# Taking the last key tile of one attention pair head by head, in a stage where TensorE hands over to a dense product

## The chip, the cores and the metric

The kernel runs on one core of one Trainium2 chip. The metric is the device time of one execution in microseconds. The kernel counts as faster or slower only beyond 2%.

## The reference

Attention with a relative-position bias, then a mixer with a low-rank token mixing and a two-layer channel product (8 batches, 8 heads, 576 tokens, 64 per head; channel width 512, hidden 2048):

```python
scores = scale * q @ k.T + bias[bucket(|i - j|)]
attn   = softmax(scores)
x      = attn @ v                      # heads side by side: 576 x 512 per batch
u      = x + (x.T @ U @ V).T
out    = u + relu(u @ w_ch1) @ w_ch2
```

## The kernel before

Two heads make a pair; g counts pairs over all batches, so g = 0 to 3 is batch 0. For each pair the scores lie in PSUM with keys on partitions, ScalarE exponentiates them into `p_sb`, VectorE multiplies the band near the diagonal by the exponentiated bias (`band`), TensorE multiplies with v (`pv`, a column of ones giving the row sums), VectorE divides (`normalise`), and TensorE mixes (`mix_t`, then `mix_ut`, which also transposes). From the fifth pair on, matmuls of the dense product (`work.run`) fill TensorE. The end of batch 0 is written out by hand, each engine taking its instructions in this order:

```python
    kts(3, 3)                        # scores and exponential of key tile 3, both heads
    to_copy = fourth_transposes()
    bands(3, 4, 0, 1)
    normalise(2)
    to_copy[0]()
    for kt in (4, 0, 1):
        pv(3, kt, (0,))
    mix_t(2, nc.scalar.copy)
    bands(3, 2)
    for kt in (4, 0, 1):
        pv(3, kt, (1,))
    bands(3, 3)
    pvs(3, 2, 3)                     # tile 2 head 0, tile 2 head 1, tile 3 head 0, tile 3 head 1
    mix_ut(2, nc.scalar.copy)
    normalise(3)
    ready[0] = True
    work.run(0.64)                   # three matmuls of the dense product
    to_copy[1]()
    mix_t(3, nc.scalar.copy)
    mix_ut(3, nc.vector.tensor_copy)
    # ... then the loop over g = 4 to 31; in it, at g = 7, segment 0:
            work.even(...)                   # dense matmuls
            # ...
            pair_transposes(g + 1, 0)        # needs the q of batch 2, all four token tiles
```

The softmax here doesn't subtract the row's maximum and nothing guards it: scores larger than these inputs give would overflow.

## Time and profile before

| | before |
|---|---|
| time, first three runs | 409.9 us median (409.36 to 410.46) |
| profiled span | 408.0 us |
| TensorE / VectorE / ScalarE / GpSimd busy | 95% / 60% / 51% / 31% |
| stage: start of pair 2's mixing product to start of pair 3's | 34.51 to 37.34, 2.83 us |
| TensorE back in the dense product | 39.53 us |
| TensorE's wait for the q load of batch 2 | 1.30 us, ending at 70.68 us |

TensorE is the busy engine, but a share doesn't say which stretch sets the end. The chain of waits does: the prediction shows that up to 70.68 us it runs through transfers and GpSimd, and through TensorE only afterwards. Below, "the mark" is the start of pair 2's mixing product, just ahead of the edit, and "the stage" runs from the mark to the start of pair 3's mixing product. TensorE's timeline has both ends of the stage, and just ahead of the second end a dense matmul (the third of `work.run(0.64)`) that waits for ScalarE's copy of pair 2's `uT`:

```profile
34.51 0.44 PE L647 MATMUL acc<-xp,upad 128*128 128x128 bf16 x5
...
37.12 0.38 PE L372 MATMUL acc<-uT,w1b 128*128 128x512 bf16 x1 [0.24 <-ACT uT L704]
37.34 0.44 PE L647 MATMUL acc<-xp,upad 128*128 128x128 bf16 x5
```

### The profile page before, as it was taken

Reading aid. Unit: us, or ns where it says so; the run is one execution under the profiler, and the core shown is the slowest. Engines: PE = TensorE matmul, PEld = TensorE weight load, DVE = VectorE, ACT = ScalarE, POOL = GpSimd, SP = SyncE. Lnnn points to the kernel's source line nnn. Section 1 sums busy time; section 2 is a strip of 40 time slices with the busy share of each in tenths; the row PEclk is TensorE's granted clock in tenths of the full one; section 3 lists DMA queues with packets and bytes.
Section 4 is the critical chain, followed back from the end, with each engine's and each line's share of the span. In section 5 each row is a group of like instructions: output and inputs, shape, how many; then the busy total and the mean of one; then the engine's idle time right before and its main releaser. Section 6 shows DMA issues by size and latency. Waiting matters only on the chain.

```text
span 408.0 us, 9061 instructions
## 1 busy us (share of the span) xinstructions
PE 386.7 (95%) x3636; PEld 214.8 (53%) x3700; DVE 243.2 (60%) x554; ACT 207.0 (51%) x289; POOL 124.7 (31%) x179
## 2 busy tenths in 40 slices
PE   3888998999999999999999999999999999999995
PEld 1456555555555555555555555555555554444443
DVE  6867887757664675566755776568655832422321
ACT  5886644565654566557655665455555640220310
POOL 4948924454454045404540454040000000000000
PEclk9789999999999999999999999999999999999999
DMA  7999999999999599949995999499022003001012
GB/s 130 181 159 157 112 187 128 119 104 155 151 78 117 123 117 94 129 104 135 108 100 130 127 88 91 110 135 105 14 66 66 14 14 95 35 4 75 26 27 77
DMA packets 162754, 40.68 MB, mean 100 GB/s; under 512 B 151792, under 2 KB 157176, under 8 KB 162712
## 3 DMA queue, kind: packets, MB, share of 16 engines
q0 software_dynamic: 108416, 17.97, 62.2%
q1 hardware_dynamic: 53080, 21.22, 25.6%
q10 hardware_dynamic: 1216, 0.92, 0.7%
q8 instruction: 29, 0.48, 0.5%
q14 instruction: 13, 0.11, 0.1%
HBM read 37.84 MB, written 9.45 MB: 116 GB/s over the span
## 4 chain that ended last, share of the span: by engine, by line
PE 81%; DMA 10%; POOL 5%; issue 2%; DVE 1%; ACT 0%; ACTq 0%; POOLq 0%
PE acc L392 30%; PE acc L372 27%; PE o L611 10%; PE sc L524 7%; DMA w1b<-in_moe_w_ch_dram 5%; DMA w2b<-in_moe_w_ch_dram 4%; PE acc L647 2%; POOL v_bf L255 2%; POOL qb L265 1%; PE acc L663 1%; DMA qb<-in_q_dram 1%; PE sc L537 1%; PE sc L558 1%; POOL qb L255 1%; DMA gp_dram<-gp 1%
## 5 line engine op out<-in xcount | busy, mean ns | idle before, releaser
L533 ACT ACTIVATE p_sb<-sc 128x1024 bf16<-128x1024 f32 x128 | 124.6, 1021 | 101.3 <-PE sc L524 101.1
L392 PE MATMUL acc<-w2b,g 128*128 128x512 bf16 (+1 forms) x560 | 128.7, 373 | 2.3 <-DVE ob L401 0.5
L372 PE MATMUL acc<-uT,w1b 128*128 128x512 bf16 x484 | 116.3, 380 | 2.5 <-issue 0.6
L392 PEld LDWEIGHTS <-g 128*128 128x128 bf16 x592 | 55.2, 98 | 70.2 <-issue 11.7
L372 PEld LDWEIGHTS <-w1b 128*128 128x128 bf16 x576 | 53.3, 98 | 71.5 <-issue 13.1
L383 DVE TENSOR_SCALAR g<-acc 128x512 bf16<-128x512 f32 x94 | 64.7, 690 | 34.7 <-PE acc L372 31.7
L587 DVE TENSOR_TENSOR p_sb<-p_sb,eb 128x768 bf16<-128x768 bf16 (+3 forms) x160 | 69.8, 465 | 12.1 <-ACT p_sb L533 9.5
L381 ACT ACTIVATE g<-acc 128x512 bf16<-128x512 f32 x50 | 29.9, 598 | 59.8 <-PE acc L372 59.6
L611 PEld LDWEIGHTS <-p_sb 128*128 128x128 bf16 x1600 | 56.3, 98 | 6.9 <-issue 1.3
L611 PE MATMUL o<-v_bf,p_sb 128*128 128x65 bf16 x1500 | 58.3, 194 | 0.2 <-DVE p_sb L587 0.2
L401 DVE TENSOR_TENSOR ob<-acc,u_tok 128x512 f32<-128x512 f32 x32 | 22.1, 691 | 44.3 <-PE acc L392 39.4
L524 PE MATMUL sc<-qkT 64*128 64x512 bf16 x256 | 41.7, 395 | 1.3 <-ACT qkT L469 0.7
L914 POOL COPY gate<-xp 1x2 bf16<-1x2 bf16 x18 | 3.1, 175 | 121.7 <-DVE xp L636 121.7
L671 DVE TENSOR_TENSOR u_tok<-acc,xp 128x512 bf16<-128x512 f32 x32 | 22.1, 691 | 24.8 <-PE acc L663 24.7
L636 DVE TENSOR_TENSOR xp<-o,rcp 128x320 bf16<-128x320 f32 x60 | 29.5, 491 | 3.2
L255 POOL DMA_DIRECT2D v_bf<-in_v_dram x32 | 28.5, 915 | 2.0 <-DMA w1b<-in_moe_w_ch_dram 1.7
L255 POOL DMA_DIRECT2D qb<-in_q_dram x24 | 22.1, 921 | 5.0 <-DVE p_sb L587 5.0
L255 POOL DMA_DIRECT2D qb<-in_k_dram x24 | 21.9, 910 | 5.5 <-DMA w2b<-in_moe_w_ch_dram 3.5
L567 ACT ACTIVATE p_sb<-sc 128x640 bf16<-128x640 f32 x32 | 22.4, 698 | 0.4 <-PE sc L561 0.3
L550 ACT ACTIVATE p_sb<-sc 128x512 bf16<-128x512 f32 x32 | 19.1, 598 | 3.5 <-PE sc L537 1.2
L634 DVE RECIPROCAL rcp<-o 128x5 f32<-128x5 f32 x60 | 11.5, 191 | 14.0 <-PE o L611 13.3
L647 PEld LDWEIGHTS <-upad 128*128 128x128 bf16 x160 | 11.4, 98 | 7.8 <-DVE xp L636 0.7
(90 smaller groups left out, 257.5 us busy)
## 6 DMA issues: line engine op xcount, KB each, us to landing
out_dram<-ob SPq DMA_DIRECT2D x32, 256.0 KB, 2.3
v_bf<-in_v_dram POOLq DMA_DIRECT2D x32, 128.0 KB, 5.7
qb<-in_q_dram POOLq DMA_DIRECT2D x27, 128.0 KB, 4.4
qb<-in_k_dram POOLq DMA_DIRECT2D x27, 128.0 KB, 4.5
w1b<-in_moe_w_ch_dram POOLq DMA_DIRECT2D x2, 1024.0 KB, 9.3
w2b<-in_moe_w_ch_dram POOLq DMA_DIRECT2D x2, 1024.0 KB, 12.5
stage<-gp_dram SPq DMA_DIRECT2D x4, 192.0 KB, 4.6
qkT<-qb SPq DMA_TRANSPOSE x40, 5.0
```

The lines of the kernel that those rows point to most:

```text
L255: nc.gpsimd.dma_start(out=dst, in_=src[b, :, t * 128 : (t + 1) * 128, :].rearrange("h p d -> p h d"),)
L372: nc.tensor.matmul(gp_, lhsT=w1b[:, ct, nt * 128 : (nt + 1) * 128], rhs=rhs[:, ct, :], start=(ct == 0), stop=(ct == 3),)
L381: nc.scalar.activation(g[:, nt, :], gp_, AF.Relu)
L383: nc.vector.tensor_relu(out=g[:, nt, :], in_=gp_)
L392: nc.tensor.matmul(op[:, c0:c1], lhsT=g[:, nt, tt * 128 : (tt + 1) * 128], rhs=w2b[:, nt, c0:c1], start=(nt == 0), stop=(nt == NHT - 1), s ...
L401: nc.vector.tensor_tensor(out=ob[:, c0:c1].rearrange("p (a c) -> p a c", c=128), in0=op[:, c0:c1].rearrange("p (a c) -> p a c", c=128), in ...
L524: nc.tensor.matmul(sp[:, hh, :], lhsT=kT[rows, i * 128 : (i + 1) * 128], rhs=qT[rows, 0:S0], start=True, stop=True,)
L533: nc.scalar.activation(P[:, i, :, 0:S0], sp, AF.Exp, scale=scale)
L567: nc.scalar.activation(P4[:, 0:SP], sp.rearrange("p a c -> p (a c)")[:, 0:SP], AF.Exp, scale=scale,)
L587: nc.vector.tensor_tensor(out=t, in0=t, in1=e, op=ALU.mult)
L611: nc.tensor.matmul(o[:, qt * 66 : qt * 66 + 65], lhsT=lhs[:, c0 : c0 + 128], rhs=rhs, start=(kt == NKT and qt == 0), stop=(kt == NKT - 1), ...
L636: nc.vector.tensor_tensor(out=xo[:, :, hh], in0=o[:, :, 0:64], in1=rbc, op=ALU.mult)
```

## The change

The intent: exponentiate head 0 first, so that its band, PV and normalising can begin while head 1's scores are still in ScalarE, and put the mixing transpose of pair 2 in between. The core of the diff:

```diff
-            def post():
-                nc.scalar.activation(P[:, i, :, 0:S0], sp, AF.Exp, scale=scale)
+            def post(hh=slice(0, 2)):
+                nc.scalar.activation(
+                    P[:, i, hh, 0:S0], sp[:, hh, :], AF.Exp, scale=scale
+                )
+            if extra:
+                return [lambda hh=hh: post(hh) for hh in (slice(0, 1), slice(1, 2))]
 # ... band() takes a slice of heads in the same way ...
-    kts(3, 3)
+    last = score(3, 3, True)
+    for post in last:
+        post()
 # ...
-    bands(3, 3)
-    pvs(3, 2, 3)
-    mix_ut(2, nc.scalar.copy)
-    normalise(3)
+    for hh in range(2):
+        pv(3, 2, (hh,))
+        band(3, 3, slice(hh, hh + 1))
+        pv(3, 3, (hh,))
+        normalise(3, (hh,))
+        if hh == 0:
+            mix_ut(2, nc.scalar.copy)
```

More of the change, by code (lines that the diff above doesn't have):

```diff
@@ L574, in score, with band @@
         return post
-    def band(g, kt):
+    def band(g, kt, hh=slice(0, 2)):
         pr = g % NPAIR
@@ L581, in band @@
             d0 = q0 - (128 * kt - 128)
-            t = p_sb[g % 2][:, kt, :, q0:q1]
-            e = eb[:, 2 * pr : 2 * pr + 2, d0 : d0 + q1 - q0]
+            t = p_sb[g % 2][:, kt, hh, q0:q1]
+            e = eb[:, 2 * pr + hh.start : 2 * pr + hh.stop, d0 : d0 + q1 - q0]
         else:
```

## The prediction

> **What bounds the kernel now.** I first read the page's engine shares and its 40 slices. TensorE is busy 95% of 408.0 us, and full from the third slice on. A local change counts only if it moves the point from which TensorE runs without a gap to the end.
>
> ```profile
> span 408.0 us, 9061 instructions
> ...
> PE 386.7 (95%) x3636; PEld 214.8 (53%) x3700; DVE 243.2 (60%) x554; ACT 207.0 (51%) x289; POOL 124.7 (31%) x179
> ```
>
> The second view is the chain that ended last, cut to 28 to 72 us, because the edited code runs from about 33 to 39 us (columns: start, length, what).
>
> ```profile
> 29.68 8.12 DMA w1b<-in_moe_w_ch_dram
> ...
> 40.95 4.61 POOL qb L265 x7
> ...
> 47.67 14.56 DMA w2b<-in_moe_w_ch_dram
> 62.24 0.30 issue
> 62.54 2.59 POOL qb L255 x3
> 65.13 5.50 DMA qb<-in_q_dram
> 70.63 0.05 issue
> 70.68 0.29 PE acc L498 x2
> ```
>
> The chain doesn't pass through the edited stage. From 29.68 to 70.63 us it consists of weight loads, GpSimd issuing loads one after another, and the q load of batch 2. Only at 70.68 us does it enter TensorE, and from there it stays on it nearly to the end. So TensorE must have slack before that point, and TensorE's waits between 33 and 80 us give its size:
>
> ```profile
> PE acc L498 <- DMA qb<-in_q_dram: 1.3, 1, 1.3
> ```
>
> TensorE stood still 1.3 us for that load. Whatever moves TensorE between 39 and 70 us by less than 1.3 us in the late direction, or by any amount in the early one, changes this wait and not the end. One entry of GpSimd's waits worried me: 5.0 us at 57.98 us put down to a VectorE band product, which would couple the loads to the compute. The instruction list has only a DMA semaphore on that load, the one of the transfer issued eight earlier: the first half of the second weight matrix. The next load (62.54 us) waits likewise for its second half. The loads are pinned by transfers; the named engine had long been done.
>
> Third, the timeline of the edited stage, TensorE and VectorE separately (start us, length us, engine line op out<-in xcount, idle before):
>
> ```profile
> 35.24 0.31 PE L611 MATMUL o<-v_bf,p_sb 128*128 128x65 bf16 x5
> 35.39 0.32 PE L611 MATMUL acc<-v_bf,p_sb 128*128 128x65 bf16 x5
> 35.55 0.31 PE L611 MATMUL o<-v_bf,p_sb 128*128 128x65 bf16 x5
> 35.70 0.32 PE L611 MATMUL acc<-v_bf,p_sb 128*128 128x65 bf16 x5
> ...
> 37.34 0.44 PE L647 MATMUL acc<-xp,upad 128*128 128x128 bf16 x5
> ```
>
> ```profile
> 34.37 0.95 DVE L587 TENSOR_TENSOR p_sb<-p_sb,eb 128x768 bf16<-128x768 bf16 x2
> 35.89 0.20 DVE L634 RECIPROCAL rcp<-o 128x5 f32<-128x5 f32 x1 [0.57 <-PE o L611]
> 36.12 0.49 DVE L636 TENSOR_TENSOR xp<-o,rcp 128x320 bf16<-128x320 f32 x1
> 36.53 0.18 DVE L634 RECIPROCAL rcp<-acc 128x5 f32<-128x5 f32 x1
> 36.75 0.49 DVE L636 TENSOR_TENSOR xp<-acc,rcp 128x320 bf16<-128x320 f32 x1
> ```
>
> VectorE does the last two band products in 0.95 us, idles 0.57 us until head 0's last PV group ends at 35.86, and normalises both heads by 37.24. The mixing product that needs this starts at 37.34. The stage is bound by PV, then VectorE, not by the exponential: it starts at 33.63 and ends at 34.66, while TensorE reaches the key tile's PV only at 35.55, with no wait there.
>
> [...]
>
> **The change part by part.**
> *Exponential.* One activation of 1024 becomes two of 512. By the trace 2 x 0.60 - 0.10 = 1.10 us in place of about 1.03: ScalarE's following copy of the next q and cast of tt begin 0.07 to 0.1 us later. The cast's result is then there at about 35.5. Head 0's half ends near 34.23 instead of 34.66, but VectorE is busy until about 34.9 with normalising pair 2 and the band of tile 2. The gain has no taker.
> *Band.* 128x640 (485 ns) becomes two of 128x320, each estimated at about 0.31 us from 298 ns at 256 elements and a slope of about 0.46 ns per element (early ones here are nearer 275). One more instruction on VectorE. What matters is that the second is now behind head 0's normalising.
> *PV and mixing on TensorE.* No matmul is added or removed. Head 1's five matmuls of tile 2 no longer stand before head 0's last five, so head 0 finishes 35.55 - 35.39 = 0.16 us earlier, at about 35.70. Then the mixing transpose of pair 2 (five matmuls) moves in front of head 1's PV. It needs tt at about 35.5, and TensorE reaches it about 35.57, so it doesn't stall and fills a hole.
> *VectorE's new order.* Before: reciprocal 0, normalise 0, reciprocal 1, normalise 1, without a wait between. After: reciprocal 0, normalise 0, band of head 1, wait for TensorE, reciprocal 1, normalise 1. Working it out: reciprocal 0 at 35.73; normalise 0 at 35.96 (0.23 later, as now); band of head 1 at 36.37 (0.41 later, as now between normalise and reciprocal), done about 36.68. In head 1's last PV group only the last three of five matmuls touch columns which that band product writes. They run after it: about 0.06 us from the release, then 0.26 us to the end of three, so 37.0. Reciprocal 1 at 37.03, normalise 1 from 37.25 to 37.74, against 37.24 before.
> *Sum in the stage.* +0.50 us at the mixing product of pair 3 (37.34 becomes about 37.84), as -0.16 for the early start and +0.66 for band, PV and hand-over inside VectorE's sequence. What follows (tt cast, transpose of pair 3, its copy, and the return to the dense stream at 39.53) is an unchanged series and shifts to about 40.03. TensorE stands idle about 0.35 us before head 1's last matmuls and saves the 0.24 us wait for the ScalarE copy of uT.
> *Sum at the end.* TensorE reaches 70.68 us with 1.30 - 0.50 = about 0.8 us of waiting left, and the load decides as before. Effect on the time: 0.0 us.
>
> **The rivals.**
> 1. The stage shortens, as the edit intends: VectorE starts normalising earlier and TensorE has mixing work to put in between. For it: the 0.57 us idle before the first reciprocal. Against it: the second band then sits on the path. Even if it gained 0.5 us, the 1.3 us wait would become 1.8: the time stays at 409.9.
> 2. The local loss isn't absorbed, because the load at 65.13 us depends on compute after all, or shifted DMA transposes of the mixed tiles (issued from 59.92 us[...]) delay it. For it: DMA share is above 0.9 in most of these slices and the load takes 5.5 us where its kind has a median of 4.4. Against it: bytes and issue order are the same, and the GpSimd semaphores are those of transfers. Full cost: 409.9 + 0.5 = 410.4.
> 3. The loss is more than the slack, because a moved wait is longer than I think, for instance an accumulator buffer not free. To show it must pass 1.3 us, 2.6 times my estimate; a stage loss of 2 us would give 410.6. I checked the buffers: the three accumulators are taken in the same order as before, and the one for pair 3's mixing is freed by head 1's normalising, which it needs anyway.
>
> **Range and chances.** The centre is the time of before, 409.9. The three runs of before spread from 409.36 to 410.46, and I add little for rivals 1 to 3, whose whole reach is under 1 us: 409.1 to 410.9. Two per cent is 8.2 us, some sixteen times the local effect, so within 2% gets 0.98, the rest split evenly.
>
> **What would show it.** In the changed profile: two 128x512 exponentials of about 0.60 us in place of one near 33.6; a 128x320 band product between the two normalisings; first reciprocal near 35.7, last normalising ending near 37.7; the dense stream returning about 40.0 instead of 39.53; TensorE's wait for the q load near 70.7 down to about 0.8 us with the load still landing near 70.6; everything after it in place. The prediction is wrong if that wait is gone or the landing has moved by more than 0.5 us. The stage working is wrong if the dense stream returns earlier than 39.5.

## The result, and the profile after

Six runs of the changed kernel have a median of 409.11 us (408.44 to 410.42), six of the kernel before beside them 410.12 (408.77 to 410.46). The ratio is 0.9984, with a 95% interval of 0.9963 to 1.0005: the same. (A ratio is the mean time of one kernel's fast runs over that of the other's of the same rounds, so not quite the ratio of the medians.) The median lies at the very bottom of the predicted range of 409.1 to 410.9, inside it by 0.01 us.

The chain of the changed kernel between 28 and 72 us (start us, length us, what):

```profile
29.30 8.06 DMA w1b<-in_moe_w_ch_dram
...
47.25 14.53 DMA w2b<-in_moe_w_ch_dram
61.78 0.30 issue
62.08 2.60 POOL qb L255 x3
64.68 5.41 DMA qb<-in_q_dram
70.09 0.05 issue
70.13 0.28 PE acc L498 x2
```

It is the chain of before, link by link, but already 0.38 us earlier at its first line, ahead of anything that was edited, and 0.54 us earlier where it reaches TensorE. The span is 0.5 us shorter. From the restart of TensorE to the end it is 407.5 - 70.13 = 337.37 us, before 408.0 - 70.68 = 337.32. So nothing after the load got shorter: the half microsecond came in with the early loads.

TensorE's waits of the changed kernel from 33 to 80 us have the load's wait at half its size:

```profile
PE acc L498 <- DMA qb<-in_q_dram: 0.6, 1, 0.6
```

The stage in the timeline, TensorE and then VectorE:

```profile
34.13 0.44 PE L652 MATMUL acc<-xp,upad 128*128 128x128 bf16 x5
...
35.37 0.39 PE L701 MATMUL acc<-ident,xp 128*128 128x128 bf16 x4
35.60 0.38 PE L616 MATMUL acc<-v_bf,p_sb 128*128 128x65 bf16 x7
36.37 0.27 PE L616 MATMUL acc<-v_bf,p_sb 128*128 128x65 bf16 x3 [0.40 <-DVE p_sb L592]
36.47 0.81 PE L372 MATMUL acc<-uT,w1b 128*128 128x512 bf16 x3
37.45 0.45 PE L652 MATMUL acc<-xp,upad 128*128 128x128 bf16 x5 [0.17 <-DVE xp L641]
```

```profile
35.36 0.20 DVE L639 RECIPROCAL rcp<-o 128x5 f32<-128x5 f32 x1 [0.58 <-PE o L616]
35.59 0.49 DVE L641 TENSOR_TENSOR xp<-o,rcp 128x320 bf16<-128x320 f32 x1
35.99 0.32 DVE L592 TENSOR_TENSOR p_sb<-p_sb,eb 128x320 bf16<-128x320 bf16 x1
36.67 0.20 DVE L639 RECIPROCAL rcp<-acc 128x5 f32<-128x5 f32 x1 [0.36 <-PE acc L616]
36.90 0.49 DVE L641 TENSOR_TENSOR xp<-acc,rcp 128x320 bf16<-128x320 f32 x1
```

Between the two normalisings VectorE now has head 1's band (35.99) and a wait of 0.36 us for the three matmuls that need it; TensorE in turn stands 0.40 us before those three, and 0.17 us more before pair 3's mixing product. The stage is 37.45 - 34.13 = 3.32 us, against 2.83.

### The profile page after: what moved, and what is told of

Same layout as the page of the kernel before. It is cut to its first block, busy times and chain, and to the rows that moved or that the text cites. A ratio compares the mean times of both kernels' runs of the same rounds, so it can differ in the third digit from the quotient of the medians.

```text
span 407.5 us, 9127 instructions
## 1 busy us (share of the span) xinstructions
PE 390.4 (96%) x3700; PEld 214.8 (53%) x3700; DVE 243.4 (60%) x555; ACT 206.9 (51%) x290; POOL 124.9 (31%) x179
## 4 chain that ended last, share of the span: by engine, by line
PE 82%; DMA 10%; POOL 5%; issue 1%; DVE 1%; ACT 1%; ACTq 0%; POOLq 0%
PE acc L392 31%; PE acc L372 28%; PE o L616 10%; PE sc L524 7%; DMA w1b<-in_moe_w_ch_dram 4%; DMA w2b<-in_moe_w_ch_dram 4%; PE acc L652 2%; POOL qb L265 2%; POOL v_bf L255 2%; PE acc L668 1%; DMA qb<-in_q_dram 1%; PE sc L542 1%; PE sc L563 1%; DMA gp_dram<-gp 1%; POOL qb L255 1%
## 5 line engine op out<-in xcount | busy, mean ns | idle before, releaser
L533 ACT ACTIVATE p_sb<-sc 128x1024 bf16<-128x1024 f32 (+1 forms) x129 | 124.6, 1015 | 100.5 <-PE sc L524 100.4
L392 PE MATMUL acc<-w2b,g 128*128 128x512 bf16 (+1 forms) x592 | 133.0, 374 | 0.5 <-DVE ob L401 0.5
L372 PE MATMUL acc<-uT,w1b 128*128 128x512 bf16 x512 | 119.5, 380 | 0.3 <-DVE uT L709 0.3
```

The costliest lines, as they stand in the source:

```text
L372: nc.tensor.matmul(gp_, lhsT=w1b[:, ct, nt * 128 : (nt + 1) * 128], rhs=rhs[:, ct, :], start=(ct == 0), stop=(ct == 3),)
L392: nc.tensor.matmul(op[:, c0:c1], lhsT=g[:, nt, tt * 128 : (tt + 1) * 128], rhs=w2b[:, nt, c0:c1], start=(nt == 0), stop=(nt == NHT - 1), s ...
L533: nc.scalar.activation(P[:, i, hh, 0:S0], sp[:, hh, :], AF.Exp, scale=scale)
```

## The experiments

The theory to test: the edit makes the stage 0.5 us longer, and the time doesn't show it, because TensorE has to wait for the q load of batch 2 anyway. The rivals: the change truly gains (0.9984 would be 0.65 us); or nothing is absorbed and the loss is regained elsewhere.

This table has what was read in the fourteen profiles, in us. "Load issue" is when GpSimd issues the awaited q load, counted from the mark. "Restart to end" starts at the fourth transposing matmul of that q, the first that needs the load. The span is printed to 0.1 us, so differences taken from it hold to about 0.05 us, whatever their second decimal.

| profile | mark at | stage | load issue | wait for the load | restart to end | span |
|---|---|---|---|---|---|---|
| before | 34.51 | 2.83 | 30.62 | 1.30 | 337.32 | 408.0 |
| changed | 34.13 | 3.32 | 30.55 | 0.64 | 337.37 | 407.5 |
| e1, before again | 33.84 | 2.83 | 30.58 | 1.21 | 337.38 | 407.3 |
| e2, changed again | 35.23 | 3.33 | 29.63 | none | 337.35 | 407.8 |
| e3, before + fill | 34.07 | 2.83 | 30.14 | none | 335.99 | 406.5 |
| e4, changed + fill | 34.68 | 3.33 | 31.02 | none | 335.98 | 407.6 |
| e5, before + 5 matmuls | 35.03 | 2.82 | 30.71 | 0.19 | 337.35 | 408.5 |
| e6, before + 20 matmuls | 33.59 | 2.83 | 31.16 | none | 337.30 | 409.9 |
| e7, exponential alone | 34.10 | 2.83 | 30.66 | 1.34 | 337.40 | 407.7 |
| e8, PV order alone | 33.93 | 2.82 | 30.68 | 1.10 | 337.31 | 407.2 |
| e9, order without exponential | 35.67 | 3.33 | 29.32 | none | 337.32 | 408.2 |
| e10, bands first | 33.75 | 2.75 | 30.57 | 1.34 | 337.33 | 407.2 |
| e11, bands first + fill | 34.17 | 2.75 | 30.57 | none | 336.06 | 406.6 |
| e12, before + fill again | 34.66 | 2.83 | 30.52 | none | 336.01 | 407.1 |

(Where there was no wait, the fourth matmul is taken 0.17 us after the first of the four, three steps of 0.055: in e2 the four start at 70.28 us and the next matmul at 70.50.)

**e1: the kernel before, no edit, as a control.**

> The kernel before, unchanged, as a control for the noise. Every theory: ratio 1.000 to its twin, and the interval shows what five rounds can resolve (I expect about 0.2% to each side). The profile should show 2.83 us from the start of pair 2's mixing product to that of pair 3's, a wait of TensorE for the q load of batch 2 near 1.3 us, give or take the half microsecond by which the early loads move from run to run, and 337.4 us from the landing of that load to the end.

Measured: ratio 0.9994 (0.9977 to 1.0011), so five rounds resolve about 0.17%, 0.7 us, to each side. Stage 2.83, wait 1.21, and the load landed at 69.87 us where it had been 70.63. An unedited kernel thus moves its landing by more than the 0.54 us that separates before and changed.

**e2: the changed kernel, no further edit.**

> The changed kernel, unchanged, repeated. Absorbed (my theory): ratio within noise of 1.000, the stage 3.32 us as in its first profile, a wait for the q load near 0.8 us left, and 337.4 us from landing to end. Rival, the change truly gains (the first six runs gave 0.9984): ratio again near 0.998, so about 0.65 us faster, and something after the landing would have to be shorter, 336.8 us or less.

Measured: ratio 1.0009 (0.9986 to 1.0031). The first ratio's 0.65 us did not come back, and restart to end is again 337.35, so the rival of a true gain falls. But the expected wait of 0.8 us was missing altogether: TensorE arrived later than the load. Its mark lies at 35.23 us, 1.1 us later than in the first profile, while the load's issue is only 0.18 us later. The stretches of the profile just ahead of the mark show why (columns: stretch, its length, busy us and count of each engine, granted clock, then two DMA columns that aren't used here):

```profile
27.00:30.40 3.40, 2.01 (x21) 1.10 (x20) 0.58 (x3) 3.31 (x6) 2.09 (x3) 0.95 1.37 91
30.40:33.50 3.10, 3.04 (x42) 2.45 (x44) 3.06 (x8) 1.57 (x2) 3.10 (x5) 0.51 0.74 92
```

The granted TensorE clock was 0.51 for these three microseconds; in the first profile of the changed kernel it was 1.00 in the same stretch. Five PV matmuls in it take 0.27 us from start to start instead of 0.155. From the third group of PV matmuls of pair 2 (at 30.41 us here, 30.30 in the first profile) to the mark it is 4.82 us here, 3.83 there and 4.22 in e4 (from 30.46 us), both at a granted clock of 1.00. What sets off such a dip is not shown: e4 had TensorE busy for the same 2.01 us between 27.00 and 30.40 us, and its clock stayed at 1.00 in the next stretch. In the first profile of the kernel before, such a stretch lies at 16 to 20 us (0.50); in e9's at 20 to 24 us (0.50); e2 has the early one (0.57 at 16 to 20 us) and this one. So a dip just ahead of the stage (0.6 to 1.0 us in e2) can decide how late TensorE comes to it, and with that how much slack there is before the load. It is not the only thing that does: e3 has none up to the mark (1.00 from 4 to 36 us), and its load is issued 30.14 us after it.

**e3 and e4: 8 dense matmuls (1.73 us) drawn forward into the hole, in both kernels.**

```diff
                 work.run(2.2)
+            if g == 7 and seg == 0:
+                work.run(1.73)
             for p in box:
```

> The kernel before with 8 matmuls of the dense product (1.73 us) drawn forward into the hole before the q load is needed. Slack theory: TensorE's wait for the q load vanishes, and those 8 matmuls are missing later, so the end comes about 1.3 us earlier than before (ratio about 0.997) and 336.1 us or less lie between landing and end. If the wait is not a true hole (something else, say VectorE or ScalarE, holds the stretch up), the time stays at 1.000.

> The same 8 matmuls drawn forward in the changed kernel. Slack theory: the hole is only about 0.8 us there, because the edited stage is 0.5 us longer, so the end comes only about 0.8 us earlier than the unfilled kernels; counted from the start of pair 2's mixing product to the end of the kernel it should be 0.5 us longer than the kernel before with the same fill: the loss that the load hides becomes visible. Rival, the loss is made up elsewhere: the two filled kernels take the same from that point to the end.

Measured: e3 has 0.9982 (0.9965 to 0.9998) and e4 0.9994 (0.9978 to 1.0010), to the kernel before. The wait for the load is gone in both. Counted from the mark to the end it is 406.5 - 34.07 = 372.43 us in e3 and 407.6 - 34.68 = 372.92 in e4, against 373.49 and 373.37 unfilled. With the hole filled, the edited kernel is 0.49 us longer than the other (up to the first q transpose, free of the span's rounding, it is 36.77 us against 36.27): the loss that the load hides is there at its full size. The rival that it is regained elsewhere falls. Against the unfilled kernels the gain of 1.06 and 0.45 us falls short of the expected 1.3 and 0.8. Of the 1.73 us drawn forward only 337.32 - 335.99 = 1.33 came off the rest; TensorE's waits in e3 show a new one shortly after the restart (e4 has it too, at L715):

```profile
PE acc L710 <- DVE ob L401: 0.3, 1, 0.3
```

**e5 and e6: 5 and 20 more matmuls right behind the stage.** The first matmul of pair 3's mixing transpose is repeated into the same accumulator, which it clears each time, so the result is right.

```diff
-        nc.tensor.matmul(tp, lhsT=tt, rhs=vpad[:, 0:S0], start=True, stop=False, ...)
+        for _ in range(1 + (5 if g == 3 else 0)):        # e6: 20
+            nc.tensor.matmul(tp, lhsT=tt, rhs=vpad[:, 0:S0], start=True, stop=False, ...)
```

> The kernel before with the first matmul of pair 3's mixing transpose given six times in place of once: 5 more matmuls of 0.216 us, so TensorE comes 1.08 us later out of the edited stage. Slack theory: absorbed by the 1.3 us wait, which falls to about 0.2 us; ratio 1.000, and 337.4 us from the landing of the q load to the end. Rival, nothing absorbs: 1.08 us slower, ratio 1.0026, the wait still near 1.3 us because the load moves with the compute.

> The same with 20 more matmuls, 4.32 us. Slack theory: 1.3 us are absorbed and about 3.0 us come out at the end, ratio about 1.0073, no wait for the q load left. Rival, nothing absorbs: 4.3 us, ratio 1.0105. Rival, DMA or another engine bounds well past the load: clearly less than 3 us.

Measured: e5 has ratio 0.9995 (0.9978 to 1.0013), e6 1.0077 (1.0058 to 1.0096), about 3.1 us. From the mark to the first of the four q transposes it is 35.60 us in e5 and 38.84 in e6, against 34.53 before: delays of 1.07 and 4.31. The e5 wait that is left:

```profile
PE acc L498 <- DMA qb<-in_q_dram: 0.2, 1, 0.2
```

So the first 1.1 us of a delay vanish and of 4.3 us about 3.1 come out, as a slack of 1.3 us says. "Nothing absorbs" wanted 1.0026 and 1.0105, and both lie outside the intervals.

**e7: the split exponential alone.** The end of the stage is as before; only `last = score(3, 3, True)` and its loop stay.

> The split exponential alone: two activations of 512 in place of one of 1024, everything after it as in the kernel before. By my working it has no taker: the stage (pair 2's mixing product to pair 3's) stays 2.83 us, to within 0.05; the pair of activations takes 1.09 us as in the changed kernel. Rival: the later cast of tt pushes TensorE, then the stage grows by about 0.07 us or more.

Measured: stage 2.83. ScalarE's line in its timeline:

```profile
33.22 1.09 ACT L533 ACTIVATE p_sb<-sc 128x512 bf16<-128x512 f32 x2
```

The split costs ScalarE 1.09 us in place of 1.03, and neither cost nor gain gets into the stage.

**e8: PV of head 0 before head 1, alone.**

```diff
     bands(3, 3)
-    pvs(3, 2, 3)
+    for hh in range(2):
+        for kt in (2, 3):
+            pv(3, kt, (hh,))
     mix_ut(2, nc.scalar.copy)
```

> The kernel before with one edit: head 0's last two PV groups before head 1's, nothing split and the mixing transpose left where it was. The -0.16 us of my sum alone: the stage falls from 2.83 us to about 2.67, first reciprocal 0.16 us earlier. The time stays at that of before (the wait for the load grows by the same 0.16 us).

A miss. The first reciprocal is 35.16 - 33.93 = 1.23 us after the mark, 0.15 earlier than before (1.38), as expected, and the last normalising ends 0.15 earlier. But the stage is 2.82. TensorE's lines say why:

```profile
36.54 0.38 PE L372 MATMUL acc<-uT,w1b 128*128 128x512 bf16 x1 [0.24 <-ACT uT L704]
36.75 0.44 PE L647 MATMUL acc<-xp,upad 128*128 128x128 bf16 x5
```

The mixing product comes behind a dense matmul which waits 0.24 us for ScalarE's copy of pair 2's `uT`. The kernel before has the same wait at 37.12 us, and its mixing product follows the freed matmul after 0.22 us, while VectorE's normalising was done at 37.24. Two chains thus ended within some tenth of a microsecond, VectorE's normalising and, last, ScalarE's copy. Shortening VectorE's alone gave nothing.

**e9: band, PV and normalising per head, but one exponential of 1024.** The changed kernel with `kts(3, 3)` put back.

> Band, PV and normalising per head as in the changed kernel, but one exponential of 1024. By my working the whole +0.50 us comes from the order on VectorE, so the stage is 3.32 us as in the changed kernel. Rival: the two parts act together (the exponential per head is what lets head 0 go first), then it differs from 3.32 by over 0.1 us.

Measured: stage 3.33. The three matmuls that wait for head 1's band are there as in the changed kernel:

```profile
37.92 0.27 PE L616 MATMUL acc<-v_bf,p_sb 128*128 128x65 bf16 x3 [0.34 <-DVE p_sb L592]
```

So the order makes the whole loss and the split exponential none of it. Here too the wait for the load was gone: the mark is at 35.67 us, and the load's issue is only 29.32 us after it.

**e10: the changed kernel with both bands ahead of PV.**

```diff
     for hh in range(2):
-        pv(3, 2, (hh,))
         band(3, 3, slice(hh, hh + 1))
+    for hh in range(2):
+        pv(3, 2, (hh,))
         pv(3, 3, (hh,))
```

> The changed kernel with both per-head band products put ahead of PV, everything else of the change kept. If the second band behind the first normalising is the cause of the longer stage, the stage (pair 2's mixing product to pair 3's) falls from 3.32 us to about 2.97, as VectorE no longer has band and hand-over between the two normalisings and only waits for head 1's PV behind the mixing transpose. If the split exponential or the mixing transpose ahead of head 1's PV is the cause, it stays near 3.3. The time stays at that of before.

The cause is right and the size a miss: stage 2.75, not 2.97. VectorE's timeline:

```profile
35.21 0.49 DVE L641 TENSOR_TENSOR xp<-o,rcp 128x320 bf16<-128x320 f32 x1
35.72 0.20 DVE L639 RECIPROCAL rcp<-acc 128x5 f32<-128x5 f32 x1
```

The second reciprocal follows the first normalising after 0.51 us, so head 1's PV was done by about then. The expected 2.97 us had VectorE waiting for that PV, and there was no such wait: from the start of the mixing transpose to that of the PV it took only 35.22 - 34.78 = 0.44 us. With the transpose moved forward, ScalarE's copy of `uT` starts early too (1.67 us after the mark, 1.97 before), so both chains of e8 are shorter, and the stage is 0.08 us shorter than before.

**e11 and e12: e10 with the fill, and e3 once more.**

> Both per-head bands ahead of PV (stage 2.75 us in its first look) together with 8 matmuls drawn forward. Counted from pair 2's mixing product to the end: 372.4 us as the kernel before with the fill, less the 0.08 us by which its stage is shorter, so 372.35; about 1.1 us less than before, ratio about 0.997. Rival: the longer transposing order gives the gain back later, then 373.4 us as before.

> The kernel before with the 8 matmuls drawn forward, repeated on another chip or at another time. If its gain is real the ratio is again below 1, near 0.9975, and 372.4 us lie between pair 2's mixing product and the end; if the first 0.9982 was luck, the ratio is about 1.000.

Measured: from the mark to the end 372.43 us in e11 and 372.44 in e12, within 0.01 of e3, each about 1.05 less than before. But the whole times don't confirm it: e11 has 0.9990 (0.9976 to 1.0004) and e12 0.9997 (0.9974 to 1.0019). Of the fills, only e3's interval excludes 1, and by the test written down for e12, a ratio near 1.000 means that e3's 0.9982 was luck. That filling the hole shortens the tail is shown in the profiles; that it makes a faster kernel is not established at this noise. The 0.08 us of e10's stage can't be told in e11 from reading error.

## Why the prediction was right

**That the time stays.** Right, for the reason given: the chain runs through the load, and e3 to e6 measure the slack from both sides. The wait that was left in the first profile is 0.64 us and not the 0.8 of the forecast: the stage took 0.49 of the 1.30, and the landing came 0.16 us earlier from the mark (35.96 against 36.12). The centre of 409.9 was 0.8 us high for the first six runs; the repeat had 409.75. That the first six still fell inside the range, by 0.01 us, is luck. The two ratios, 0.9984 and 1.0009, lie on both sides of 1.

**The stage's sum.** Counted from the mark, with the predicted value in brackets: first reciprocal 1.23 us (1.22), head 1's band 1.86 (1.86) lasting 0.32 (0.31), the last three PV matmuls 2.24 (2.23), second reciprocal 2.54 (2.52), end of normalising 3.26 (3.23), mixing product 3.32 (3.33), dense stream 5.52 (5.52). TensorE's idle time before the three matmuls was 0.40 (0.35), and its 0.24 us wait for ScalarE's copy is gone, as predicted. Two exponentials took 1.09 us (1.10, twice 0.60 less 0.10: in the profile of before one of 512 elements takes 598 ns on average, one of 1024 takes 1021, and two of 1024 together take 1.94 us where twice 1.02 is 2.04). The slope of 0.46 ns per element, from which the band's 0.31 was estimated, comes from 298 ns at 256 elements and 417 at 512 in the same profile. That the mixing product agrees to 0.01 us is partly luck: VectorE ended 0.03 us later than worked out, and the hand-over to TensorE took 0.06 us where the working kept the 0.10 of before, a figure that came from the ScalarE chain of e8.

**GpSimd's odd entry.** The 5.0 us of idle time that the profile of before puts down to a VectorE band product, I took for the wait for a transfer. That the named engine "had long been done" is not shown there: its two band products ran from 56.95 to 57.90 us, and the load was issued at 57.98. In GpSimd's waits of the two profiles, the same wait of the same load reads, before and then changed (waiting line, who released it: us in total, times, longest us):

```profile
POOL qb L255 <- DVE p_sb L587: 5.0, 1, 5.0
```

```profile
POOL qb L255 <- DVE u_tok L676: 5.0, 1, 5.0
```

The length stays and the named instruction changes. In e5's profile the same wait is put down to the transfer itself, in one line with the wait for the second half of the same weights (4.9 and 3.5 us):

```profile
POOL qb L255 <- DMA w2b<-in_moe_w_ch_dram: 8.5, 2, 4.9
```

e6 settles it: with the compute 4.3 us later from the stage on, the awaited load is still issued at 64.75 us. The prediction's "the GpSimd semaphores are those of transfers" leaves one out: the `gate` copy at 58.85 us, among these loads, reads VectorE's `xp`. It had no wait there, nor in e6 (57.56 us), so it did not hold the loads up.

**What was wrong.** Three things. First, the step "TensorE stood still 1.3 us" was taken as a fixed slack. It depends on the execution: in e2 and e9 there was none, and by the prediction's own test ("wrong if that wait is gone") e2, the changed kernel once more, counts against it. With the awaited landing about 5.4 us after its issue (5.50 before, 5.41 changed, 5.36 in e5), I estimate that e2's hole without the edit would have been 0.3 us, so that some 0.2 us of the loss came out at the end; in e9, by the same estimate, the hole would have been 0.1 us or less, and most of the loss came out. The noise of the times is too wide to show either. In e2 the late mark comes from the clock dip just ahead of the stage (0.6 to 1.0 us more for the same work than at a granted clock of 1.00). In e9 the dip comes earlier and goes together with a late mark; that it is the only cause there is not shown. Second, the other half of that test, "the landing has moved by more than 0.5 us", was a bad one: it moved by 0.54 us, and so did that of an unedited kernel (0.76 in e1). The absolute times that I gave (first reciprocal 35.7, dense stream 40.0) were off by the same early shift; all distances from the mark agreed to 0.03 us. Third, "the stage is bound by PV, then VectorE" named one of two chains, and not the one that ended last; e8 found the other, ScalarE's copy of `uT`. It hardly mattered for the sum, as the edit makes VectorE's chain the longer one by half a microsecond.

## What to carry to other kernels

Before you shorten or lengthen a stage, find the next place where its engine waits for something that the stage doesn't feed: that wait can pay for a loss (here for all of e5's 1.07 us of delay, and for about 1.2 of e6's 4.31), and a few dummy matmuls measure how much it can pay. That it takes up a gain in the same way was my estimate; no time here shows it. Look at it in more than one profile: the changed kernel had a wait of 0.64 us in one execution and none in another. When work is split per head, look at what the split puts between two instructions that ran back to back on the engine that ends the stage. Compare profiles by distances from a point just ahead of the edit, not by absolute times, and look at the granted clock ahead of that point (0.51 in e2).
